# Block attention and two MLPs on one core: where the weights are converted, where s and b are applied, and how the first softmax is normalised

## Chip, cores and metric

The kernel runs on one core of a Trainium2 chip. The metric is the device time of one execution in microseconds. Before the change it is 1034.1 us, the median of three runs (1032.76 to 1035.13).

## What is computed

Attention in blocks of 64 positions (4 batches, 8 heads, 576 positions, head size 64), whose output of 2304 tokens by 512 passes through two MLPs with 2048 hidden columns. The weights arrive as float64 words and are used as fp32.

```python
scores = scale * q @ k.T; masked where block_i < block_j; attn = softmax(scores)
x = attn @ v                                   # 2304 tokens x 512
h = x @ w_in;  g = s * relu(h)**2 + b;  x = g @ w_out        # first MLP, s and b are scalars
h = x @ w_in2; g = max(0.01 * h, h);    out = g @ w_out2     # second MLP
```

## The kernel before, in words

Nothing is kept in bf16: every fp32 operand of the MLPs is split into a high part (rounded to the type `float32r`) and a low part (the rest), and each product is three matmuls: high by high, low by high, high by low. Tokens are cut into five groups of positions, k = 0 to 4 (four of 128 positions by 4 batches, 512 columns, and one of 64 by 4, 256 columns). A block is one group through one MLP; ten blocks run in the order 0, 1, 2, 4, 3 for the first MLP and 0, 1, 2, 3, 4 for the second (`ORDER`). A block has 16 units (`NF`), one for each 128 hidden columns, and a unit is `m_in` (12 matmuls into the PSUM bank `h`), four element-wise operations on ACT and DVE, and `m_out` (12 matmuls into the four banks `y0` to `y3`).

The order of the work is written by a planner: `Graph.add` registers a step with the engines that it may run on and a cost for each, its predecessors, the buffers that it opens and uses, and a due time; `Graph.order` simulates the engines and always starts the ready step with the earliest due time that has its buffers. The steps are then issued in that order, so each engine's queue, SP's for the DMAs included, is a fixed sequence. A step that may run on several engines goes to the first that is idle in that simulation, DVE before ACT. `port=True` keeps two such steps from overlapping on DVE and POOL.

Attention of the first group runs ahead of everything, as four head pairs: two scores banks per pair, `softmax` (L382: maximum, exp with its sum, reciprocal, and one normalising multiplication per column group, L422, on POOL or DVE), `transposed` (L436, through the one bank `t`) and the product with v into the bank `s`. The attention of each later group (`later_block`, L541) is spread over the block before it, in 16 units of one head pair and one batch.

First weights (`first_weights`, L301): each chunk f has two halves of 512 KB, w_in and w_out. Chunks 0 to 14 load both halves as words into a buffer of the pool `w` (L312), chunk 15 through the single buffer `raw` (L320). `convert` (L259) turns a half into fp32 in a buffer `u` of the pool `st`: ACT scales the high words (L264), DVE shifts (L268), puts in the sign (L272) and the low bits (L278), all with a contiguous result. `split` (L288) makes the high part on ACT (L290) and the low part on POOL or DVE (L293). Second weights (`second_weights`, L327): during blocks 0 to 3, half by half through `raw` and `u`, stored to DRAM as fp32 (`w2s`, L340), and loaded again (L348) and split while block 4 and block 5 run. The 16 buffers of the pool `w` hold raw first words, the first weights and then the second weights.

In the first MLP (L703 to L711) a unit's four operations are Relu on ACT, `s * r * r` on DVE with the scalar read from `s_sb`, `+ b` with the rounding to the high part on ACT with the scalar from `b_sb`, and the low part on DVE with `b_sb` again. `h` has one bank in the first MLP and three (`s`, `s`, `t`) in the second. `x_split` (L661) splits a block's input; for the second MLP it loads it from `yT`, which the first MLP's outputs were written to.

Of the kernel before, what the change touches and what calls it, by code (L numbers as in the profile page):

```python
# [43 lines left out]
class Graph:  # L44
# [22 lines left out]
    def order(self):  # L67
# [90 lines left out]
def act(n, ptr=0, acc=False):  # L158
    return 0.19 + n / 1200 + 0.09 * ptr + 0.2 * acc
# [15 lines left out]
def kernel(  # L175
# [23 lines left out]
    scale = 1.0 / float(D) ** 0.5  # L199
    EARLY = NF - 1  # L200
# [4 lines left out]
    def ps(name, bufs):  # L205
# [5 lines left out]
        "w": (sb("w", NF), NF), "st": (sb("st", 3), 3), "raw": (sb("raw", 1), 1),  # L211
# [3 lines left out]
        "sm": (sb("sm", 8), 8),  # L215
# [3 lines left out]
    G = Graph({k: n for k, (_, n) in pools.items()}, ("k", "v", "p", "pt", "s", "t", "h", "xf", "xh", "xl", "st", "raw"))  # L219
# [8 lines left out]
    id_sb = const.tile([128, 128], F32, name="id_sb")  # L228
    s_sb = const.tile([128, 1], F32, name="s_sb")
# [3 lines left out]
    w2s = dr_p.tile([NF, 2, 128, 512], F32, name="w2s")  # L233
# [3 lines left out]
    att_pe = [16 * (share[k] * 1.64e-3 + 2 * (k + 1) * 0.16 + 0.2) for k in range(NB)]  # L237
# [21 lines left out]
    def convert(raw, view, loaded, due):  # L259

        u = buf("st", [128, 512], F32, "u")

        def up(e):
            e.activation(out=u(), in_=view()[:, :, 1].bitcast(F32), func=ACTF.Copy, scale=2.0 ** -112)  # L264

        def shift(e):
            ui = u().bitcast(I32)
            e.tensor_scalar(out=ui, in0=ui, scalar1=3, scalar2=None, op0=ALU.logical_shift_left)  # L268

        def sign(e):  # L270
# [5 lines left out]
        def low(e):
            ui = u().bitcast(I32)
            e.scalar_tensor_tensor(  # L278
                out=ui, in0=view()[:, :, 0], scalar=29, in1=ui, op0=ALU.logical_shift_right, op1=ALU.bitwise_or
            )  # L280

# [539 lines left out]
```

## Time and profile before

| | us |
|---|---|
| median of three runs | 1034.1 (1032.76 to 1035.13) |
| the profiled execution | 1033.27 |
| its span | 1031.4 |
| PE busy | 996.7 |
| DVE busy | 484.6 |
| ACT busy | 392.6 |
| POOL busy | 144.1 |

The span is the stretch that the profile covers, 1.9 us shorter than the execution's own time. Busy time is the union of an engine's instructions. Matmuls are pipelined and their ends are modelled, so a busy PE can still be one that goes slowly: how long a block takes tells more. L695 and L734 are the MLPs' matmuls, L430 and L602 the scores, L445 the transposes, L639 and L519 the products with v.

### The profile page before, as it was taken

How to read it: one execution, taken by the hardware profiler on the slowest of the kernel's cores; microseconds unless marked ns; L12 is line 12 of the kernel's file. 1: busy time of each engine (PE TensorE's matmuls, PEld its weight loads, DVE VectorE, ACT ScalarE, POOL GpSimd, SP SyncE). 2: the span in 40 equal slices, each digit the busy share in tenths (PEclk: the TensorE clock that was granted, in tenths of full speed). 3: DMA queues.
4: the chain of work that ended last, by engine and by line, in shares of the span. 5: the costliest groups of instructions: out<-in, count | busy, mean ns of one | idle time of the engine just before them, and what ended most of it. 6: DMA issues, size and time to landing. Idle time of an engine off the chain costs nothing.

```text
span 1031.4 us, 14803 instructions
## 1 busy us (share of the span) xinstructions
PE 996.7 (97%) x5520; PEld 810.6 (79%) x5520; DVE 484.6 (47%) x956; ACT 392.6 (38%) x893; POOL 144.1 (14%) x268
## 2 busy tenths in 40 slices
PE   6799998999999999999999999999999999999997
PEld 5577776787777777777788888888888888888897
DVE  4688877656666676567664544113111211311221
ACT  4555654434444443355443445123212211321221
POOL 3445543101121111022220000000000000000000
PEclk8899999999999999999999999999999999999999
DMA  6455652544536656355624233001000200200011
GB/s 170 137 166 173 192 155 89 159 122 130 167 103 176 190 171 191 99 154 156 185 77 149 91 103 102 1 1 56 27 1 1 82 1 1 62 1 1 1 41 22
DMA packets 97607, 100.66 MB, mean 98 GB/s; under 512 B 29312, under 2 KB 72448, under 8 KB 97536
## 3 DMA queue, kind: packets, MB, share of 16 engines
q1 hardware_dynamic: 95904, 99.19, 32.7%
q8 instruction: 44, 0.72, 0.3%
q10 hardware_dynamic: 1632, 0.52, 0.2%
q14 instruction: 27, 0.22, 0.1%
HBM read 81.86 MB, written 17.83 MB: 97 GB/s over the span
## 4 chain that ended last, share of the span: by engine, by line
PE 90%; DVE 3%; ACT 2%; DMA 2%; POOL 1%; SPq 1%; issue 1%; ACTq 0%; DVEq 0%; POOLq 0%
PE h L695 37%; PE y L734 37%; PE s L430 5%; PE t L445 4%; PE o L639 4%; PE s L602 2%; DMA early<-in_moe_w_in_dram 1%; POOL p L422 1%; ACT g L706 1%; DMA fq<-in_q_dram 1%; DVE pt L372 0%; DVE g L707 0%; DVE u L272 0%; SPq L561 0%; ACT p L408 0%
## 5 line engine op out<-in xcount | busy, mean ns | idle before, releaser
L695 PE MATMUL h<-xh,w 128*128 128x512 f32 (+1 forms) x1280 | 452.9, 384 | 4.4 <-ACT g L706 3.2
L734 PE MATMUL y<-gh,w 128*128 128x512 f32 (+1 forms) x1280 | 372.4, 374 | 4.0 <-ACT gh L709 3.2
L695 PEld LDWEIGHTS h<-xh,w 128*128 128x128 f32 x1280 | 237.7, 189 | 56.6 <-ACT g L706 8.8
L734 PEld LDWEIGHTS y<-gh,w 128*128 128x128 f32 x1280 | 230.4, 189 | 47.6 <-ACT gh L709 5.0
L734 PE MATMUL y<-gl,w 128*128 128x512 f32 (+1 forms) x640 | 237.0, 370 | 0.5 <-DVE gl L715 0.2
L695 PE MATMUL h<-xl,w 128*128 128x512 f32 (+1 forms) x640 | 236.1, 369 | 0.0
L715 DVE TENSOR_TENSOR gl<-g,gh 128x512 fp32r<-128x512 f32 (+1 forms) x80 | 51.1, 639 | 294.8 <-ACT g L714 294.8
L713 ACT ACTIVATE gh<-h 128x512 fp32r<-128x512 f32 (+1 forms) x80 | 44.4, 554 | 289.2 <-PE h L695 289.2
L734 PEld LDWEIGHTS y<-gl,w 128*128 128x128 f32 x640 | 120.8, 189 | 23.2 <-DVE gl L710 2.3
L695 PEld LDWEIGHTS h<-xl,w 128*128 128x128 f32 x640 | 121.1, 189 | 21.8 <-issue 2.8
L706 ACT ACTIVATE g<-h 128x512 f32<-128x512 f32 (+1 forms) x80 | 44.3, 554 | 125.2 <-PE h L695 117.3
L422 POOL TENSOR_SCALAR p<-p,l 128x64 f32<-128x64 f32 (+7 forms) x128 | 72.0, 578 | 107.3 <-DVE l L417 75.0
L707 DVE SCALAR_TENSOR_TENSOR g<-g,s_sb 128x512 f32<-128x512 f32 (+1 forms) x80 | 56.4, 705 | 57.7 <-ACT g L706 57.0
L445 PE MATMUL t<-id_sb,p 128*128 128x128 f32 x400 | 68.7, 284 | 8.6 <-DVE pt L372 3.7
L408 ACT ACTIVATE p<-s,nm 128x64 f32<-128x64 f32 (+7 forms) x128 | 62.8, 504 | 36.4 <-DVE nm L402 24.9
L445 PEld LDWEIGHTS t<-id_sb,p 128*128 128x128 f32 x400 | 49.4, 144 | 29.8 <-POOL p L422 7.4
L430 PE MATMUL s<-k,qz 128*128 128x192 f32 (+2 forms) x192 | 69.5, 466 | 2.9 <-ACT p L408 2.9
L399 DVE TENSOR_REDUCE nm<-s 128x1 f32<-128x192 f32 (+3 forms) x104 | 52.8, 522 | 30.7 <-PE s L430 30.4
L709 ACT ACTIVATE gh<-g,b_sb 128x512 fp32r<-128x512 f32 (+1 forms) x80 | 54.1, 677 | 31.0 <-DVE g L707 30.8
L710 DVE SCALAR_TENSOR_TENSOR gl<-g,b_sb,gh 128x512 fp32r<-128x512 f32 (+1 forms) x80 | 57.1, 713 | 15.0 <-ACT gh L709 14.8
L372 DVE COPY pt<-t 128x512 f32<-128x512 f32 (+2 forms) x60 | 37.5, 625 | 40.3 <-PE t L445 40.2
L293 POOL TENSOR_TENSOR w<-u,w 128x512 fp32r<-128x512 f32 x32 | 43.5, 1358 | 58.5 <-ACT w L290 52.3
(52 smaller groups left out, 718.3 us busy)
## 6 DMA issues: line engine op xcount, KB each, us to landing
raw<-in_moe_w_in_dram SPq DMA_DIRECT2D x17, 512.0 KB, 4.6
raw<-in_moe_w_out_dram SPq DMA_DIRECT2D x17, 512.0 KB, 4.0
w2s<-u SPq DMA_DIRECT2D x32, 256.0 KB, 4.4
v<-in_v_dram SPq DMA_DIRECT2D x32, 256.0 KB, 3.5
wf<-w2s SPq DMA_DIRECT2D x16, 512.0 KB, 3.6
early<-in_moe_w_in_dram SPq DMA_DIRECT2D x15, 512.0 KB, 4.1
early<-in_moe_w_out_dram SPq DMA_DIRECT2D x15, 512.0 KB, 4.2
k<-in_k_dram SPq DMA_DIRECT2D x32, 144.0 KB, 3.4
```

The source lines that it names most:

```text
L399: e.reduce_max(out=nm()[:, j:j + r], in_=i, axis=AX.X)
L408: e.activation(out=P()[:, pcols[j]:pcols[j] + n], in_=bk()[:, c:c + n], func=ACTF.Exp, bias=nm()[:, j:j + 1], scale=scale, accum_out=l()[: ...
L422: e.tensor_scalar(out=pp, in0=pp, scalar1=l()[:, j:j + 1], scalar2=1.0, op0=ALU.mult, op1=ALU.mult)
L430: e.matmul(out=bk()[:, c:c + n], lhsT=q_ap(j), rhs=k_ap(j, n), start=True, stop=True)
L445: e.transpose(tb()[:, x * 128:(x + 1) * 128], P()[:, pc:pc + 128], id_sb)
L695: e.matmul(out=h()[:, :T], lhsT=w()[:, wi, c * 128:(c + 1) * 128], rhs=x[blk, c]()[:, :T], start=(c == 0 and n == 0), stop=(c == KD - 1 an ...
L706: a = G.add({"ACT": act(T)}, lambda e: e.activation(out=g()[:, :T], in_=h()[:, :T], func=ACTF.Relu), [prev], [g], [h], due)
L707: a = G.add({"DVE": dve(T)}, lambda e: e.scalar_tensor_tensor(out=g()[:, :T], in0=g()[:, :T], scalar=s_sb, in1=g()[:, :T], op0=ALU.mult, o ...
L709: hi = G.add({"ACT": act(T, 1)}, lambda e: e.activation(out=gh()[:, :T], in_=g()[:, :T], func=ACTF.Identity, bias=b_sb), [a], [gh], [g], due)
L710: lo = G.add({"DVE": dve(T)}, lambda e: e.scalar_tensor_tensor(out=gl()[:, :T], in0=g()[:, :T], scalar=b_sb, in1=gh()[:, :T].bitcast(F32), ...
L715: lo = G.add({"DVE": dve(T)}, lambda e: e.tensor_tensor(out=gl()[:, :T], in0=g()[:, :T], in1=gh()[:, :T].bitcast(F32), op=ALU.subtract), [ ...
L734: e.matmul(out=y()[:, :T], lhsT=w()[:, wi, d * 128:(d + 1) * 128], rhs=x()[:, :T], start=(f == 0 and n == 0), stop=(f == NF - 1 and n == 2),)
```

## The change

First and second weights: a chunk's two halves are converted together, in instructions of 1024 columns, in place in the buffer of raw words (`chunk`): DVE shifts the low words, puts the sign of the high words into them, ACT scales the high words, DVE shifts them and joins the two, ACT makes the high part, DVE the low part. Low words and high words alternate in memory, so each of these reads, and all but the last two write, every second word. Chunk 0 stays in halves. Chunk 15 goes in halves through two buffers of the pool `pt`; the pool `raw` is gone. Loads of chunks 0 to 14 carry an earliest time of 6.0 + 4.9 f us for the planner. The second weights no longer go through DRAM: they are loaded and converted as `w` buffers come free in block 4, at most three chunks ahead, each due 25 us before its use.

First MLP: a unit is Relu on ACT, the square (ACT, or DVE as g * h with h from PSUM), the rounding on ACT and the low part on DVE, without scalars. s is a scale on the evacuation of the outputs. b is taken through the weights: group 4 carries two more columns, of ones in the high part and zeros in the low (set by two POOL copies per unit), its outputs there give the column sums of w_out, and b times those, `c_sb`, is added in the second MLP's `x_split`. Block 4 uses three banks for `h`.

Start: the exp table is loaded by a dummy exp, eight matmuls run on zeros ahead of the data, k is loaded before q, ACT's queue issues the loads of three pairs instead of two, the third pair's scores have banks of their own, the transposes alternate between the banks `t` and `h`, the product with v goes to `t`, the third and fourth pair's probabilities lie in a `w` buffer, and the normalisation is two `tensor_tensor` operations on DVE, of 256 and 512 columns, with the reciprocal broadcast. Further, the planner's costs change by a few hundredths of a us.

```diff
+    WARM, LATE, PACE, AHEAD = 8, 10, (6.0, 4.9), 3
...
+    def chunk(w, raw, layer, f, lds, halves, at0, due):
+        r, rr, n = slice(halves[0], halves[-1] + 1), slice(halves[0] - at0, halves[-1] + 1 - at0), len(halves)
+        parts = lambda s, dt: w().bitcast(dt).rearrange("p (i s) n -> p i s n", s=2)[:, r, s]
+        word = lambda s: raw()[:, rr, :, s]
+        def low(e):
+            e.tensor_scalar(out=word(0), in0=word(0), scalar1=29, scalar2=None, op0=ALU.logical_shift_right)
+        def sign(e):
+            e.scalar_tensor_tensor(out=word(0), in0=word(1), scalar=-(1 << 31), in1=word(0), op0=ALU.bitwise_and, op1=ALU.bitwise_or)
         def up(e):
+            e.activation(out=word(1).bitcast(F32), in_=word(1).bitcast(F32), func=ACTF.Copy, scale=2.0 ** -112)
         def shift(e):
+            e.scalar_tensor_tensor(out=word(1), in0=word(1), scalar=3, in1=word(0), op0=ALU.logical_shift_left, op1=ALU.bitwise_or)
         def hi(e):
+            e.activation(out=parts(0, F32R), in_=word(1).bitcast(F32), func=ACTF.Copy)
         def lo(e):
+            e.tensor_tensor(out=parts(1, F32R), in0=word(1).bitcast(F32), in1=parts(0, F32), op=ALU.subtract)
...
     def second_weights():
+            raw = buf("w", [128, 2, 512, 2], I32, "early")
+            lds = [w_load(1, f, i, raw, i, [opened[f - AHEAD] if f >= AHEAD else w_ok[0, NF - 1, 1]], [raw] * (i == 0), due - 6, 0) for i in range(2)]
+            opened.append(chunk(w, raw, 1, f, lds, [0, 1], 0, due))
...
     def softmax(k, banks, cols, P, pcols, due, after):
+        if k == 0:
+            for j in range(0, ns, 4):
+                def fn(e, j=j):
+                    pp = P()[:, 128 * j:128 * j + 512].rearrange("p (r n) -> p r n", r=4)[:, :, :cols[j][2]]
+                    e.tensor_tensor(out=pp, in0=pp, in1=l()[:, j:j + 4].unsqueeze(2).to_broadcast([128, 4, cols[j][2]]), op=ALU.mult)
...
     def x_split(blk, c):
+            hi = G.add({"ACT": act(T)}, lambda e: e.activation(out=h()[:, :T], in_=xf()[:, :T], func=ACTF.Identity, bias=cc), [*ok, *c_ok], [h], [xf], due)
...
     def m_in(blk, f):
-        h = bank("h" if layer == 0 else ("s", "s", "t")[f % 3], "h")
+        h = bank("h" if blk < NB - 1 else ("s", "s", "t")[f % 3], "h")
...
-            a = G.add({"DVE": dve(T)}, lambda e: e.scalar_tensor_tensor(
-                out=g()[:, :T], in0=g()[:, :T], scalar=s_sb, in1=g()[:, :T], op0=ALU.mult, op1=ALU.mult), [a, *sb_ok], [], [g], due, port=True)
-            hi = G.add({"ACT": act(T, 1)}, lambda e: e.activation(out=gh()[:, :T], in_=g()[:, :T], func=ACTF.Identity, bias=b_sb), [a], [gh], [g], due)
+            a = G.add(both(T), square, [a], uses=[g, h], due=due)
+            hi = G.add({"ACT": act(T)}, lambda e: e.activation(out=gh()[:, :T], in_=g()[:, :T], func=ACTF.Copy), [a], [gh], [g], due)
...
+            if k == NB - 1:
+                hi = G.add({"POOL": 0.15}, lambda e: e.tensor_copy(out=gh()[:, T:T + 2], in_=ones[:, 0:2]), [a, ones_ok], [], [gh], due)
+                lo = G.add({"POOL": 0.15}, lambda e: e.tensor_copy(out=gl()[:, T:T + 2], in_=ones[:, 2:4]), [hi, lo, ones_ok], [], [gl], due)
```

## Rows read from the trace of the kernel before

**Rows 1.** The page: its part 1, busy time of each engine with its share of the span and its instructions; the first line of its part 4, the chain that ended last by engine.

```profile
PE 996.7 (97%) x5520; PEld 810.6 (79%) x5520; DVE 484.6 (47%) x956; ACT 392.6 (38%) x893; POOL 144.1 (14%) x268
...
PE 90%; DVE 3%; ACT 2%; DMA 2%; POOL 1%; SPq 1%; issue 1%; ACTq 0%; DVEq 0%; POOLq 0%
```

**Rows 2.** The table by stretches: start and end in us, length, then busy us and instructions (x) of PE, PEld, DVE, ACT and POOL, the granted clock, the busy share of the DMA engines and GB/s. The borders are those at which a new block's 192 first matmuls begin.

```profile
0.00:41.00 41.00, 28.69 (x170) 22.80 (x171) 19.76 (x42) 18.10 (x76) 16.04 (x49) 0.79 0.60 164
41.00:182.80 141.80, 129.97 (x682) 97.58 (x680) 113.58 (x236) 82.75 (x192) 65.86 (x88) 0.99 0.51 153
182.80:302.10 119.30, 119.24 (x648) 94.82 (x648) 72.00 (x149) 51.11 (x112) 19.31 (x39) 1.00 0.48 138
...
542.70:628.20 85.50, 84.81 (x374) 69.80 (x374) 42.48 (x64) 37.62 (x64) 0.00 (x0) 1.00 0.33 108
628.20:715.20 87.00, 87.00 (x386) 72.06 (x385) 17.92 (x27) 24.55 (x44) 0.00 (x0) 1.00 0.08 28
```

**Rows 3.** The chain of waits inside three stretches (41 to 182.8, 302.1 to 429.9 and 429.9 to 542.7 us, in this order): the share of the stretch that each engine and line has in it.

```profile
by line: PE h L695 21.6%; PE y L734 19.8%; PE s L430 7.5%; DMA early<-in_moe_w_in_dram 6.3%; PE o L639 4.7%; PE t L445 4.2%; issue 3.2%; DVE g L707 3.0%; DVE u L272 3.0%; POOL p L422 2.8%; SPq L555 2.7%; DVE u L278 2.5%; ACT g L706 2.5%; PO
...
by line: PE h L695 34.2%; PE y L734 33.4%; PE s L602 12.3%; PE o L639 7.3%; PE t L445 7.3%; DMA qz<-in_q_dram 1.7%; POOL p L621 1.0%; ACT g L706 0.9%; SPq L561 0.8%; DVE nm L606 0.4%; issue 0.3%; DVE u L268 0.3%; DVE nm L610 0.2%
...
by line: PE y L734 24.3%; PE s L430 23.3%; PE h L695 19.7%; PE o L639 14.7%; PE t L445 12.8%; ACT g L706 1.4%; ACT pt L370 1.0%; issue 1.0%; DVE xl L678 0.6%; ACT xh L676 0.6%; DVE pt L372 0.5%; ACT p L408 0.3%; ACTq L706 0.1%
```

**Rows 4.** The timeline of the first 45 us, engine by engine (ACT, DVE, POOL, PE): start and length in us, engine, line, operation, what it writes and reads, how many in a row, and in brackets the idle time before it with what ended it.

```profile
10.69 1.28 ACT L408 ACT_TABLE_LOAD   x1 [10.69 <-DMA fq<-in_q_dram]
...
7.89 0.42 DVE L399 TENSOR_REDUCE nm<-s 128x4 f32<-128x256 f32 x1 [4.81 <-PE s L430]
...
40.27 0.69 DVE L529 TENSOR_TENSOR xl<-o,xh 128x512 fp32r<-128x512 f32 x1 [0.17 <-ACT xh L527]
...
15.42 2.58 POOL L422 TENSOR_SCALAR p<-p,l 128x64 f32<-128x64 f32 x8 [11.37 <-ACT p L408]
...
32.52 2.58 POOL L422 TENSOR_SCALAR p<-p,l 128x64 f32<-128x64 f32 x8 [1.38 <-ACT w L290]
...
5.92 6.54 PE L430 MATMUL s<-fk,fq 128*128 128x64 f32 x32 [5.92 <-DMA fq<-in_q_dram]
...
18.69 1.12 PE L445 MATMUL t<-id_sb,p 128*128 128x128 f32 x4 [0.79 <-DVE pt L372]
...
21.65 1.93 PE L430 MATMUL s<-fk,fq 128*128 128x64 f32 x14
```

**Rows 5.** Groups of instructions in block 0 (41 to 182.8 us) on DVE and POOL: line, engine, operation, tiles and shapes, count, busy us, mean ns of one, idle time before them and what ended it.

```profile
L278 DVE SCALAR_TENSOR_TENSOR u<-early,u 128x512 int32<-128x512 int32 x28 | 22.1, 790 | 0.1
...
L268 DVE TENSOR_SCALAR u<-u 128x512 int32<-128x512 int32 x29 | 14.6, 504 | 1.3 <-ACT u L264 1.3
...
L414 DVE TENSOR_SCALAR l<-l 128x2 f32<-128x2 f32 x20 | 8.6, 430 | 4.0 <-ACT p L408 4.0
L402 DVE TENSOR_SCALAR nm<-nm 128x2 f32<-128x2 f32 x21 | 7.2, 342 | 0.4
...
L293 POOL TENSOR_TENSOR w<-u,w 128x512 fp32r<-128x512 f32 x30 | 40.9, 1363 | 58.5 <-ACT w L290 52.3 <-DVE u L272 3.6 <-DMA qz<-in_q_dram 1.6
```

**Rows 6.** The tiles `early` and `u` (first weights as loaded, and their converted half): duration in ns, least, median and longest, of one instruction of a line.

```profile
L272 DVE SCALAR_TENSOR_TENSOR u<-early,u x30: 678/684/954, 29.7 to 165.3; 128x512 int32<-128x512 int32 x30
L278 DVE SCALAR_TENSOR_TENSOR u<-early,u x30: 676/684/1770, 30.4 to 166.1; 128x512 int32<-128x512 int32 x30
...
L268 DVE TENSOR_SCALAR u<-u x64: 375/420/1514, 26.4 to 517.3; 128x512 int32<-128x512 int32 x64
```

**Rows 7.** SP's queue in the timeline (start us, length, line, operation), twice two DMAs that follow each other on it.

```profile
27.90 0.51 SPq L312 DMA_DIRECT2D early<-in_moe_w_in_dram  x1
40.58 1.14 SPq L561 DMA_DIRECT2D k<-in_k_dram  x2
...
159.53 0.43 SPq L320 DMA_DIRECT2D raw<-in_moe_w_in_dram  x1
172.09 0.33 SPq L320 DMA_DIRECT2D raw<-in_moe_w_out_dram  x1
```

**Rows 8.** Groups in blocks 1 to 3 (182.8 to 542.7 us) on DVE and ACT, columns as in rows 5.

```profile
L272 DVE SCALAR_TENSOR_TENSOR u<-raw,u 128x512 int32<-128x512 int32 x32 | 25.9, 809 | 0.9
...
L278 DVE SCALAR_TENSOR_TENSOR u<-raw,u 128x512 int32<-128x512 int32 x32 | 22.9, 715 | 0.7
...
L268 DVE TENSOR_SCALAR u<-u 128x512 int32<-128x512 int32 x32 | 14.8, 463 | 6.5 <-ACT u L264 3.7 <-DMA k<-in_k_dram 2.4
...
L402 DVE TENSOR_SCALAR nm<-nm 128x2 f32<-128x2 f32 x27 | 5.5, 202 | 0.7
...
L414 DVE TENSOR_SCALAR l<-l 128x2 f32<-128x2 f32 x28 | 4.7, 166 | 9.8 <-ACT p L408 9.7
...
L264 ACT ACTIVATE u<-raw 128x512 f32<-128x512 f32 x32 | 21.2, 663 | 11.7 <-DMA raw<-in_moe_w_out_dram 5.5 <-DMA raw<-in_moe_w_in_dram 5.0 <-DMA w2s<-u 0.7
```

**Rows 9.** Groups around the border of the two MLPs (542.7 to 715.2 us) on DVE and ACT, columns as in rows 5.

```profile
L293 DVE TENSOR_TENSOR w<-wf,w 128x512 fp32r<-128x512 f32 x32 | 21.3, 688 | 6.1 <-ACT w L290 6.1
...
L707 DVE SCALAR_TENSOR_TENSOR g<-g,s_sb 128x512 f32<-128x512 f32 x16 | 12.0, 750 | 31.8 <-ACT g L706 31.8
...
L715 DVE TENSOR_TENSOR gl<-g,gh 128x512 fp32r<-128x512 f32 x15 | 10.4, 692 | 63.6 <-ACT g L714 63.6
L706 ACT ACTIVATE g<-h 128x512 f32<-128x512 f32 x16 | 9.6, 598 | 34.8 <-PE h L695 34.7
```

More of the change, by code (lines that the diff above doesn't have):

```diff
@@ L274, in sign @@
             )
[L276 to L280, printed above, removed]
-        a = G.add({"ACT": 0.66}, up, [loaded], [u], [raw], due)
-        a = G.add({"DVE": dve(512, 2)}, shift, [a], uses=[u], due=due, port=True)
-        a = G.add({"DVE": dve(512)}, sign, [a], uses=[u, raw], due=due, port=True)
-        a = G.add({"DVE": dve(512)}, low, [a], uses=[u, raw], due=due, port=True)
@@ L298, in w_tile @@
-    def w_tile(layer, f):
-        return buf("w", [128, 4, 512], F32R, "w")
+            e.tensor_tensor(out=parts(1, F32R), in0=word(1).bitcast(F32), in1=parts(0, F32), op=ALU.subtract)
+        a = G.add({"DVE": dve(512 * n, 2)}, low, lds, uses=[raw], due=due, port=True)
+        a = G.add({"DVE": dve(512 * n)}, sign, [a], uses=[raw], due=due, port=True)
+        a = G.add({"ACT": act(512 * n)}, up, [a], uses=[raw], due=due)
+        a = G.add({"DVE": dve(512 * n)}, shift, [a], uses=[raw], due=due, port=True)
@@ new lines, in chunk, with w_load @@
+        last = w_ok.get((layer, f - 1, 0)) if layer == 0 else None
+        h = a = G.add({"ACT": act(512 * n)}, hi, [a, last], [w] * (halves[0] == 0), [w, raw], due)
+        a = G.add({"DVE": dve(512 * n)}, lo, [a], uses=[w, raw], due=due, port=True)
+        for i in halves:
+            w_ok[layer, f, i] = a
+        return h
+    def w_load(layer, f, i, raw, k, after, opens, due, rel):
+        return G.add(
+            {"SP": 0.65}, lambda e: e.dma_start(out=raw()[:, k], in_=words(layer, f, i)),
+            after, opens, [raw], due, nbytes=524288, rel=rel,
+        )
@@ L432, in scores @@
             fresh.add(bk)
[L433 removed]
+            out.append(G.add({"PE": max(n * 1.67e-3, 0.214) + 0.02}, fn, after, new, [bk, *q, *kk], due - 5))
         return out
@@ L455, in transposed @@
         return done
+    tiny = G.add({"DVE": 0.1}, lambda e: memz(e, warm), due=-95)
+    G.add({"ACT": 1.4}, lambda e: e.activation(out=warm, in_=warm, func=ACTF.Exp), [tiny], due=-94)
+    wb = bank("h", "warm")
+    for i in range(WARM):
+        G.add(
+            {"PE": 0.43}, lambda e: e.matmul(out=wb()[:, :128], lhsT=qz[0][:, 0].rearrange("d h c -> d (h c)"),
+                                             rhs=qz[0][:, 0].rearrange("d h c -> d (h c)"), start=True, stop=True),
+            [qz_ok[0]], [wb] * (i == 0), [wb], -90,
+        )
     fq = [buf("w", [128, 2, B, 2, 2, 64], F32, "fq") for _ in range(2)]
```

201 lines of the change are left out of this document (98 added, 103 removed).

## The prediction

> **What bounds the kernel now.** The page first: PE is busy 97% of the span and the chain that ended last is 90% PE [rows 1], so only the places where that chain leaves PE can pay. The table by stretches finds them [rows 2]. From 542.7 us on there is almost nothing: blocks 4 and 5 take 85.5 and 87.0 us with PE busy for 84.8 and 87.0. Block 1 (182.8 to 302.1) is PE-bound too: 119.3 us, PE busy 119.24 [rows 2]. Block 0, the same 192 first matmuls and no heavier attention, takes 141.8 us, 22.5 more, and its chain is only 57.8% PE (21.6 + 19.8 + 7.5 + 4.7 + 4.2); the rest is weight loads, conversions, POOL and queue issue [rows 2, 3]. Ahead of it stand 41 us of loads and first softmax at a mean granted clock of 0.79 [rows 2]. Blocks 2 and 3 leave PE for about 5.5% and 5.0% of their chains: 7 and 5.6 us [rows 3]. So some 13 us lie in blocks 2 and 3, 22.5 in block 0, and an unknown part of 41 in the start.
>
> Durations are those of the profiled execution: 1033.27 us, 1.9 over its span of 1031.4 and 0.8 under the median of 1034.1. The sum is made on the span.
>
> **Start (0 to 41 us).** The four head pairs follow each other at 5.7 us: POOL's row of eight normalisations begins at 15.42 for the first and at 32.52 for the fourth [rows 4]. The path through a pair is exp, five of those POOL operations, four transposes, a PSUM copy, four more transposes that wait 0.8 us for that copy (one bank), AV, then the next scores, which use the banks of the pair two before. The change cuts this in four places. (a) The table load at 10.69 (1.28 us) moves ahead of the data: -1.3. (b) Eight POOL operations (2.58 us) become two on DVE. I price them by DVE's rows of the same sizes, 0.42 and 0.69, so 1.1; but the first transposes need only five of the eight (five eighths of 2.58, 1.6), so it is -0.5 per pair. (c) Two banks for the transposes: -0.8 per pair. (d) The third pair's scores go to banks of their own and no longer queue behind AV. What then sets the pace is DVE: per pair two reduces, four small operations, the norm, one or two copies and the low part, 0.42 + 0.69 + 0.8 + 1.1 + 1.0 + 0.69 = 4.7 us. Three periods of 4.7 for 5.7: -3.0; with (a) and the first pair's share of (b) and (c), -1.3: -5.6. Against it, ACT's queue now holds three more DMA issues and the early exp between its first and second issue, so the first pair's q lands later by the table load and its wait, +1.4. For it, eight warm-up matmuls: the first 32 score records take 6.54 us, 0.20 each, the later 14 take 1.93, 0.14 each [rows 4], so up to 1.9 for the first pair. I set these two against each other and take **-6** (0 if DVE, which also gets the first chunk's conversion here, keeps the old pace; -10 if all four add).
>
> **Block 0.** Each chunk of weights (two halves) costs DVE today 2 x (0.42 + 0.684 + 0.684) = 3.6 us at the median of clean instructions [rows 6] and POOL two low parts of 1.36. After, the low parts move to DVE, in instructions of 1024 columns. A clean 512-column instruction is 0.684, so 1024 columns add 512 / 0.96 = 0.53: 1.22. The one-source shift is 0.42, so 0.69 at double rate. A chunk is 0.69 + 3 x 1.22 = 4.35. DVE is busy 113.6 of 141.8 us, 80% [rows 2]. From that: some 15 us of it is excess over the clean durations (28 x 0.11 on L278, 29 x 0.08 on L268, 20 x 0.26 on L414, 21 x 0.14 on L402, and a rest on the other operations) [rows 5, 6, 8]. I read it as DVE held by POOL, whose 30 low parts run 40.9 us here, and it goes with them. That leaves 98. Conversions: 28 halves of three clean instructions, 50 us, become 14 chunks of 4.35, 61: +11. The MLP's two scalar operations, 15 x 2 x 0.75 [rows 9], become one of 0.69 and, a third of the time, a square of 0.69 (the planner may put it on ACT): -8.6. DVE's work is then 100 us, and at the same 80% share the block takes 126: **-16**. The floor is PE's own 119 (-23). The other end: the shift loses its double rate (+0.53 x 14 / 0.8 = 9) and DVE's share falls, and nothing is won (0).
>
> Two things speak for the better part of this. Loads: SP issues one at 27.90 us, then nothing at all until a key load at 40.58, and weight loads have 6.3% of block 0's chain, 9 us [rows 3, 7]. Loads are now paced by 4.9 us a chunk for the planner, ahead of a consumption of about 7.5, so the same standstill finds weights already there. And the last chunk's two halves used one buffer, loads at 159.5 and 172.1 [rows 7]; they now have two. Those two are `pt` buffers, so the next attention units wait for them a few us, behind MLP matmuls. The `h` bank is held through the square, 0.7 us longer; 12 output matmuls lie between two uses of it, 12/384 of a block's 87.0 us, 2.7, so I cost it at nothing; without that cover it would be 0.7 per unit.
>
> **Blocks 1 to 3.** Out go 32 halves of the second weights, 63.6 us of DVE and 21.2 of ACT [rows 8], and 32 loads, 32 stores and 16 reloads on SP's queue. Of the 13 us off PE in blocks 2 and 3, 2.2 are q loads and some are POOL; I take a third as conversions' share, -5. In comes a POOL copy on the path from `gl` to the output matmuls of block 3, twice 16, of two columns each: between nothing and, with a wait like a 128x2 operation of DVE at each end, 0.17 twice [rows 8], 16 x 0.34 = 5; I take +1 since units wait for PE more than for `gl`. The two extra columns are nothing. Together **-4** (0 to -10).
>
> **The MLPs' border.** All 16 second chunks are now converted between the first freed weight buffer (about 550) and 690. DVE has 42.5 + 17.9 busy of 172.5 us there [rows 2]; less 21.3 of today's low parts [rows 9] and 9 of scalar forms, plus 16 x 4.35 = 70: 100, or 58%. Spread, it is hidden: the MLP's chain of four operations (0.60 + 0.69 + 0.60 + 0.69) has the three banks that block 4 now gets. Packed one chunk per 5.44 us unit, DVE needs 4.35 + 0.69 = 5.04, still under it, but `gl` queues behind 1.22 us at a time. The loads wait on SP for freed buffers, ahead of block 5's x loads, which are due 20 us early. I take **+2** (0 to +10). The scale and the constant c sit on evacuations and x splits that exist already: nothing; c is ready 87 us before its use.
>
> **Sum:** -6 - 16 - 4 + 2 = -24. Span 1007.4, execution 1009.3, median **1010**.
>
> **Rivals.** (1) **The work only changes engine.** DVE takes the low parts over, loses the shift's double rate on the strided words, and block 0 stays near 137 to 142 us; the start and blocks 1 to 3 still pay. 1010 + 11 to 16: about 1024. For it: DVE was at 80% already. Against: POOL's holds go.
>
> (2) **Strided words in place.** The sign and the shift now read two operands and write one, all at every second word. If such streams run at half rate, each is 2 x 1.07 + 0.15 = 2.3, and with a single-rate shift a chunk is 1.22 + 2 x 2.3 + 1.22 = 7.0, 2.7 more. Block 0: 14 x 2.7 = 37 more DVE, 138 us, at 90% share 153: +11. Border: 7.0 + 0.69 = 7.7 against 5.44 per unit, 16 x 2.3 = 36 if packed, 20 with the spread. Start -4, blocks 1 to 3 -4: 1034 + 23 = 1057, slower. It decides from about 1 us more per chunk, 25%. Against it: today's sign and low operations read one such operand at 0.684, as fast as the contiguous low part of the second weights, 0.688 [rows 6, 9]. For it: no row has a strided result. [...]
>
> (3) **The gain is given back:** the border costs 10, the new order stalls elsewhere, and the time is about 1032.
>
> **How the numbers follow.** Forecast 0.6, its own range 998 to 1020; (1) 0.2; (2) 0.12; (3) 0.08, of which half lies within 0.2% (about 2 us, what a measurement here can tell from no change) and most of the rest above. Faster: 0.6 + 0.2 = 0.8; same 0.05; slower 0.15. The range reaches down to 992 (all good ends, -41, are 18 us lower and unlikely together) and up to 1036, over (1) and (3); it leaves out (2) and the best ends.
>
> **What would show it.** Fourth low part of the first block at about 35 us instead of 40.96; block 0 near 126 us with DVE near 100 busy; sign and shift at 1.22 and the one-source shift at 0.69; blocks 4 and 5 still 172 to 175 us. Wrong if those instructions last 2 us, if block 0 keeps 140, or if PE waits for `gl` at the border.

## The result, and the profile after

The changed kernel takes **1016.7 us** (median of four runs, 1014.97 to 1019.93) against 1034.0 in the same comparison: 0.984 of it [0.981, 0.987], 17 us less. Forecast were 1010, range 992 to 1036; that range takes in 1034, so a time inside it says little, and the parts of the sum have to be checked one by one. The profiled execution is the longest of the four, 1019.93 us with a span of 1018.1. Further down a second profile of the same kernel (span 1014.2) is used as the control.

The page's part 1 and the first line of its chain, as in [rows 1]; then the table by stretches, as in [rows 2], cut where a block's first matmuls begin (start, block 0, block 1, block 3, block 4, block 5).

```profile
PE 995.8 (98%) x5536; PEld 816.7 (80%) x5536; DVE 452.9 (44%) x855; ACT 403.9 (40%) x866; POOL 93.3 (9%) x238
...
PE 92%; DVE 3%; ACT 2%; DMA 1%; issue 1%; POOL 0%; ACTq 0%; SPq 0%; DVEq 0%; POOLq 0%
```

```profile
0.00:40.00 40.00, 30.64 (x181) 27.06 (x181) 23.85 (x50) 20.34 (x81) 4.32 (x17) 0.75 0.88 259
40.00:160.00 120.00, 117.07 (x629) 93.00 (x627) 95.70 (x174) 79.58 (x156) 22.91 (x48) 1.00 0.41 132
160.00:289.60 129.60, 129.46 (x713) 101.45 (x712) 56.33 (x132) 51.26 (x125) 20.47 (x48) 1.00 0.24 67
...
414.40:528.70 114.30, 110.03 (x875) 87.75 (x874) 59.36 (x141) 46.74 (x121) 27.84 (x78) 1.00 0.31 88
528.70:614.50 85.80, 85.80 (x386) 71.29 (x386) 64.64 (x79) 52.08 (x70) 0.00 (x0) 1.00 0.50 174
614.50:701.90 87.40, 87.30 (x385) 71.96 (x385) 37.30 (x48) 35.30 (x53) 0.00 (x0) 1.00 0.19 67
```

The converting instructions, as in [rows 6] (least, median and longest ns), in the order of the chain but for ACT's two:

```profile
L263 DVE TENSOR_SCALAR early<-early x31: 418/689/697, 24.4 to 636.1; 128x1024 int32<-128x1024 int32 x29, 128x512 int32<-128x512 int32 x2
L266 DVE SCALAR_TENSOR_TENSOR early<-early x31: 679/1220/1229, 25.1 to 636.9; 128x1024 int32<-128x1024 int32 x29, 128x512 int32<-128x512 int32 x2
...
L274 DVE SCALAR_TENSOR_TENSOR early<-early x31: 684/1220/1228, 29.6 to 639.3; 128x1024 int32<-128x1024 int32 x29, 128x512 int32<-128x512 int32 x2
...
L282 DVE TENSOR_TENSOR w<-early,w x31: 635/1224/1432, 32.3 to 641.7; 128x1024 fp32r<-128x1024 f32 x29, 128x512 fp32r<-128x512 f32 x2
```

That is 0.69 and three times 1.22 us, as priced. The price took 0.96 columns per ns; measured, 512 columns more take 0.536 us where two operands are read (1.220 against 0.684 [rows 6]), 0.955 per ns, and 0.269 in the one-source shift (0.689 against 0.420 [rows 6]). The fourth low part of the first block, 40.27 to 40.96 us before [rows 4], is here:

```profile
40.06 0.69 DVE L540 TENSOR_TENSOR xl<-o,xh 128x512 fp32r<-128x512 f32 x1 [0.17 <-ACT xh L538]
```

With that as the first border and block 4's first matmul (542.7 us before) as the second, the span divides like this:

| us | predicted | first profile | control |
|---|---|---|---|
| start, to the end of the fourth low part | -6 | -0.2 (40.75) | -2.6 (38.37) |
| blocks 0 to 3 from there | -16 - 4 | -13.7 (to 528.8) | -15.3 (to 524.8) |
| block 4 to the end | +2 | +0.6 | +0.7 |
| span | -24 | -13.3 | -17.2 |

Blocks 0 and 1 can't be compared by length: the new plan moves some attention from block 0 into block 1 (682 PE instructions before and 629 now, against 648 and 713). So I use **lost time**: over a stretch, the sum of the distances between the starts of successive matmuls, less the sum of the distances that the same shapes have when nothing holds them (227 ns for 512 columns of an MLP matmul, 120 for 256, and so on). With the undisturbed distances taken a little otherwise the sums shift by up to 2 us, their differences between kernels by up to 1.5. Lost time is 24.8 us before and 9.7 now in block 0, -15.1. In blocks 1, 2, 3 it was 3.5, 7.3, 9.6 and is 4.5, 5.0, 12.6: 20.4 before and 22.1 now, +1.7. The control gives the same figures within 0.1. Block 0 paid for nearly all of it: behind block 0's first matmul the span is 994.8 us before and 978.2 now, 17 less, while that matmul itself starts at 36.6 us before and at 40.0 now (36.4 in the control).

### The profile page after: what moved, and what is told of

The parts are those of the page before. It is cut to its first block, busy times and chain, and to the rows that moved or that the text cites. A ratio compares the mean times of both kernels' runs of the same rounds, so it can differ in the third digit from the quotient of the medians.

```text
span 1018.1 us, 14594 instructions
## 1 busy us (share of the span) xinstructions
PE 995.8 (98%) x5536; PEld 816.7 (80%) x5536; DVE 452.9 (44%) x855; ACT 403.9 (40%) x866; POOL 93.3 (9%) x238
## 4 chain that ended last, share of the span: by engine, by line
PE 92%; DVE 3%; ACT 2%; DMA 1%; issue 1%; POOL 0%; ACTq 0%; SPq 0%; DVEq 0%; POOLq 0%
PE h L716 38%; PE y L765 37%; PE s L430 6%; PE o L650 4%; PE t L445 4%; PE s L613 2%; PE o L530 1%; ACT p L400 1%; DVE nm L391 0%; DVE g L732 0%; POOL p L422 0%; DMA fk<-in_k_dram 0%; ACT g L734 0%; ACT w L279 0%; DMA fq<-in_q_dram 0%
## 5 line engine op out<-in xcount | busy, mean ns | idle before, releaser
L765 PE MATMUL y<-gh,w 128*128 128x512 f32 (+2 forms) x1280 | 369.4, 372 | 0.1
L765 PE MATMUL y<-gl,w 128*128 128x512 f32 (+2 forms) x640 | 236.2, 369 | 0.2 <-DVE gl L745 0.2
L745 DVE TENSOR_TENSOR gl<-g,gh 128x512 fp32r<-128x512 f32 (+1 forms) x80 | 51.0, 638 | 271.5 <-ACT g L744 271.5
L716 PEld LDWEIGHTS h<-xl,w 128*128 128x128 f32 x640 | 121.0, 189 | 21.3 <-issue 2.6
L422 POOL TENSOR_SCALAR p<-p,l 128x192 f32<-128x192 f32 (+3 forms) x95 | 59.0, 634 | 189.5 <-DVE l L409 136.0
L732 DVE TENSOR_TENSOR g<-g,h 128x512 f32<-128x512 f32 (+1 forms) x52 | 32.8, 630 | 64.2 <-ACT g L734 63.8
L358 ACT ACTIVATE pt<-t 128x512 f32<-128x512 f32 (+2 forms) x67 | 33.7, 502 | 64.6 <-PE t L445 63.9
L360 DVE COPY pt<-t 128x512 f32<-128x512 f32 (+2 forms) x53 | 34.0, 641 | 52.0 <-PE t L445 51.6
L737 DVE TENSOR_TENSOR gl<-g,gh 128x512 fp32r<-128x512 f32 (+1 forms) x80 | 51.0, 637 | 11.7 <-ACT gh L736 10.2
L736 ACT ACTIVATE gh<-g 128x512 fp32r<-128x512 f32 (+1 forms) x80 | 47.1, 588 | 16.1 <-DVE g L732 14.6
```

Source lines behind the costliest of these rows:

```text
L422: e.tensor_scalar(out=pp, in0=pp, scalar1=l()[:, j:j + 1], scalar2=1.0, op0=ALU.mult, op1=ALU.mult)
L716: e.matmul(out=h()[:, :T], lhsT=w()[:, wi, c * 128:(c + 1) * 128], rhs=x[blk, c]()[:, :T], start=(c == 0 and n == 0), stop=(c == KD - 1 an ...
L736: hi = G.add({"ACT": act(T)}, lambda e: e.activation(out=gh()[:, :T], in_=g()[:, :T], func=ACTF.Copy), [a], [gh], [g], due)
L737: lo = G.add({"DVE": dve(T)}, lambda e: e.tensor_tensor(out=gl()[:, :T], in0=g()[:, :T], in1=gh()[:, :T].bitcast(F32), op=ALU.subtract), [ ...
L745: lo = G.add({"DVE": dve(T)}, lambda e: e.tensor_tensor(out=gl()[:, :T], in0=g()[:, :T], in1=gh()[:, :T].bitcast(F32), op=ALU.subtract), [ ...
L765: e.matmul(out=y()[:, :W], lhsT=w()[:, wi, d * 128:(d + 1) * 128], rhs=x()[:, :W], start=(f == 0 and n == 0), stop=(f == NF - 1 and n == 2),)
```

## Experiments

Each is an edit of the changed kernel. Since the start of one and the same kernel varies by some 4 us from run to run (block 0's first matmul at 40.0 and at 36.4 us), the table gives what can be read apart from it: the end of the fourth low part, the lost time in block 0 and in blocks 1 to 3, and the span behind block 0's first matmul, which the first profile and the control have at 978.2 and 977.8.

| run | median us | ratio to before | 4th low part | lost, block 0 | lost, 1 to 3 | span behind |
|---|---|---|---|---|---|---|
| e0_after (control) | 1017.0 | 0.983 [0.981, 0.985] | 38.4 | 9.7 | 22.1 | 977.8 |
| e2_no_warm | 1016.7 | 0.983 [0.981, 0.986] | 40.0 | | | 977.8 |
| e3_third_first | 1014.6 | 0.981 [0.978, 0.983] | 39.0 | 9.5 | 21.6 | 977.1 |
| e1_hold | 1021.3 | 0.987 [0.985, 0.989] | 43.6 | | | 978.7 |
| e1b_hold_few | 1015.6 | 0.983 [0.981, 0.984] | 35.2 | | | 977.8 |
| e7b_lo_on_pool | 1028.2 | 0.994 [0.992, 0.996] | 40.2 | 19.1 | 22.2 | 987.5 |
| e10_late_loads | 1058.5 | 1.024 [1.022, 1.027] | 42.4 | 49.7 | 21.7 | 1019.2 |
| e4b_square_gg | 1016.7 | 0.983 [0.982, 0.985] | 38.9 | 10.3 | 18.5 | 975.2 |
| e5_no_b | 1018.4 | 0.985 [0.984, 0.987] | 39.4 | 9.6 | 21.3 | 977.2 |
| e6_second_before | 1017.0 | 0.984 [0.982, 0.987] | 40.4 | 9.5 | 21.2 | 977.1 |
| e8_sb_in_unit | 1017.4 | 0.984 [0.982, 0.986] | 40.2 | 9.3 | 21.0 | 976.5 |
| e9_hold_and_square | 1012.2 | 0.980 [0.978, 0.981] | 36.3 | 10.4 | 18.4 | 974.9 |

The medians come from three sets of runs, in which the kernel before took 1034.8 us (e0 to e3 and e1_hold), 1033.9 (e1b, e4b, e5, e7b) and 1032.9 (e6, e8, e9, e10). Across sets only the ratios can be compared, and a microsecond between two medians there says nothing.

### The start

Three theories of why the start gained so little: the order of the work on TensorE (A), TensorE's granted clock, which is 0.50 from 13.5 to 23.7 us of the first profile (B), VectorE and the loads (C).

**Control**

> The changed kernel once more, word for word, as the kernel to compare the next ones with on the same chip. Every theory expects 1015 to 1020 us; its start (to the first m_in matmul) 40 us, block 0 about 120 us, blocks 1 to 3 about 369 us together. If the clock sets the spread between executions, the start's length here goes with the length of its half-clock stretches: 20 us of them gave a start of 40.0 us in the first profile.

Same time, but another start: 36.4 us to the first m_in matmul instead of 40.0. TensorE's timeline at the first scores, in the first profile and in the control:

```profile
5.75 5.86 PE L430 MATMUL s<-fk,fq 128*128 128x64 f32 x32 [0.87 <-DMA fq<-in_q_dram]
```

```profile
5.36 2.02 PE L430 MATMUL s<-fk,fq 128*128 128x64 f32 x16 [0.58 <-DMA fq<-in_q_dram]
8.65 2.03 PE L430 MATMUL s<-fk,fq 128*128 128x64 f32 x16 [1.27 <-DMA fq<-in_q_dram]
```

In the control they start 112 ns apart from the first on. In the first profile the first 20 are 214 ns apart and the rest 112, with the same warm-up ahead, and the clock's column (last but two) does not show it:

```profile
0.00:13.00 13.00, 9.64 (x48) 9.18 (x48) 4.46 (x9) 3.94 (x18) 3.98 (x15) 1.00 0.72 178
```

The column counts time without an entry in the trace's list of clock changes as full speed. The first entry of that list, full speed, begins at 10.05 us in the first profile, where the 21st score matmul starts, and at 4.53 us in the control, ahead of all scores.

**No warm-up**

```diff
-    WARM, LATE, PACE, AHEAD = 8, 10, (6.0, 4.9), 3
+    WARM, LATE, PACE, AHEAD = 0, 10, (6.0, 4.9), 3
```

> The changed kernel without its eight warm-up matmuls. Theory B expects the first scores at half clock from the first matmul on, the first exponential 1 to 2 us later and the start 1 to 2 us longer; theories A and C expect the start within 1 us, since the first loads set the first scores and the third pair's exponentials the end.

Its first 20 score matmuls are 214 ns apart, the first exponential starts at 10.2 us, as in the first profile (10.5) and 1.8 later than in the control (8.4). The median is the control's. So the warm-up saves about 2 us up to the first exponential in an execution in which it works, and it does not always work: of the twelve profiles with it, the first exponential starts at 8.4 to 8.5 us in eight and at 10.2 to 10.5 in four.

**Third pair's scores first**

```diff
-        tr = transposed(P, pcols, cells, pt, nrm, due, ("t", "h"))
+        tr = transposed(..., also=first_sc[2][1][-1:] if p == 0 else [])   # all scores planned ahead of this loop
```

> The changed kernel with one change of order in the start: the 18 score matmuls of the third pair of heads are put ahead of the first pair's transposes on TensorE, so they don't wait for the first pair's softmax. Theory A (the third pair's scores stand behind the first pair's transposes in TensorE's order, so ScalarE has nothing to exponentiate from 19.5 to 24.25 us): the third pair's exponentials start at 18 to 20 us instead of 24.74, the fourth low part of the first block is done 3 to 5 us earlier than 40.06, and the time falls by 3 to 5 us. Theory B (the half clock of TensorE in the start costs it): the idle time before the first transposes shrinks, the clock may stay up longer, but the start shortens by 1 to 2 us only. Theory C (loads and VectorE set the pace): the fourth low part stays at 40 us within 1 us, and the time with it.

The third pair's exponentials do start at 17.5 us instead of 23.1, but the first pair pays: its low part starts at 22.5 instead of 19.4, and the fourth ends at 39.0 instead of 38.4. Theory A falls. The median is 2.4 us under the control's, with overlapping intervals; whether that is a gain stays open.

**TensorE kept busy**

```diff
+        if p == 0:   # behind the second pair's scores
+            for i in range(12): matmul(out=wb()[:, :128], lhsT=zz(), rhs=zz())
+        if p == 2:   # behind the third pair's scores (first trial only)
+            for i in range(24): matmul(out=wc()[:, :128], lhsT=zz(), rhs=zz())
```

> The changed kernel, its order otherwise kept, with 36 matmuls of no use in TensorE's gaps of the start (12 behind the second pair's scores, 24 as filler behind the third pair's), so that TensorE is not idle from 11.6 to 14.4 us. Theory B (the half clock of 13.5 to 23.7 us costs the start): the granted clock stays at full speed there, the groups of transposes, scores and AV behind it run in half their time (t 2.2 to 1.1, s 4.1 to 2.05, o 2.0 to 1.0 us), and the start falls by 3 to 5 us. Theory A (order) and theory C (loads, VectorE): the clock stays up but the start changes by less than 1 us, since ScalarE's and VectorE's chains set it. If the filler stands in the way, the start grows by up to 36 x 0.06 = 2 us.

A miss of the experiment's making: the 24 fillers read a buffer that a q load writes, waited for that load, and held the third pair's transposes until 33.5 us. Up to there it went as theory B says: second low part at 23.8 instead of 26.4. So again, with the first twelve alone:

> The changed kernel with twelve matmuls of no use on TensorE behind the second pair's scores, and none of the 24 fillers that the first trial of this had. Theory B (the half clock of 13.5 to 23.7 us costs the start): the clock stays up until about 20 us, the second low part of the first block comes 2 to 3 us earlier than at 26.4, as it did with the fillers (23.8), the fourth at 35 to 36 instead of 37.7, and the time is 1014 to 1015 us. Theory C (VectorE, which is busy without a gap from 26 us on, sets the end of the start): the second low part comes earlier, the fourth stays at 37 to 38 us, and the time is 1016 to 1018 us.

The stretch of 16 to 22 us (length, busy us of PE, PEld, DVE, ACT, POOL, then granted clock, DMA) in the first profile and in this one:

```profile
16.00:22.00 6.00, 6.00 (x36) 5.55 (x35) 2.80 (x7) 1.19 (x2) 0.15 (x1) 0.50 0.90 277
```

```profile
16.00:22.00 6.00, 5.84 (x58) 5.23 (x54) 3.82 (x10) 3.27 (x17) 0.15 (x1) 1.00 0.92 288
```

At a granted clock of 0.50 TensorE gets through 36 matmuls, at 1.00 through 58. Ahead of it, it had been idle from 11.6 to 14.4 us in the first profile, and its granted clock fell to 0.50 at 13.5. The fourth low part ends at 35.2 us, 3.2 before the control's: theory B is shown for this execution. Of the 3.2 us, 2.0 are won up to the first low part and 1.2 on the way to the second; from there on the low parts follow each other as in the control (5.8 and 5.6 us against 5.7 and 5.6). And the profiled execution is the fastest of four that spread from 1012.9 to 1016.9 us: by the ratios (0.983 and 0.983) the median gains nothing.

For theory C, the last part of the start, up to the fourth low part, in the control and before:

```profile
26.00:38.37 12.37, 8.67 (x60) 6.66 (x61) 11.91 (x25) 9.54 (x28) 0.00 (x0) 0.86 0.86 259
```

```profile
26.00:41.00 15.00, 11.41 (x68) 7.96 (x67) 9.11 (x21) 7.70 (x25) 6.84 (x20) 0.66 0.45 150
```

VectorE is busy for 96% of it now and was for 61%: it took over GpSimd's normalising and low parts, and some 7 us of conversions stand in its row there. What they hold up can be read at the fourth pair in the control: its product with v, its high part and its low part, and what stands ahead of these two on ScalarE and VectorE.

```profile
34.78 1.15 PE L530 MATMUL o<-pt,fv 128*64 128x128 f32 x16
...
35.70 1.17 ACT L271 ACTIVATE early<-early 128x1024 f32<-128x1024 f32 x1
...
36.55 1.22 DVE L266 SCALAR_TENSOR_TENSOR early<-early 128x1024 int32<-128x1024 int32 x1
...
36.72 0.64 ACT L538 ACTIVATE xh<-o 128x512 fp32r<-128x512 f32 x1
...
37.68 0.69 DVE L540 TENSOR_TENSOR xl<-o,xh 128x512 fp32r<-128x512 f32 x1
```

The product is done at 35.93 us, the high part starts 0.8 us later, behind a conversion on ScalarE, and the low part 0.3 us after the high part's end, behind one on VectorE: 1.1 us of the start are seen to go to conversions here. Fewer conversions in this stretch were seen in e10_late_loads alone, where the fourth pair's product with v was put behind the first m_in matmuls and ended later; so how much of the start the conversions cost in all is not settled.

### Block 0

```diff
-        a = G.add({"DVE": dve(512 * n)}, lo, [a], uses=[w, raw], due=due, port=True)
+        on = {"POOL": pool(512 * n, True)} if layer == 0 and f % 2 else {"DVE": dve(512 * n)}
+        a = G.add(on, lo, [a], uses=[w, raw], due=due, port=True)
```

> The changed kernel with the low parts of every second chunk of the first weights on GpSimd (1024 columns each, seven of them in block 0), as all of them were before in halves. Theory (GpSimd's operations hold VectorE, and that was block 0's loss): 7 x 2.7 = 19 us of GpSimd come back, half of what was there; VectorE's other operations get longer by some 7 us in all while its own work falls by 8.5; block 0 grows by 4 to 10 us, the time to 1021 to 1027. Rival (earlier loads and whole chunks are what paid, and the low parts' engine is of no weight): block 0 stays within 2 us of 120.

Block 0: 130.0 us, lost time 19.1 instead of 9.7, the span behind its first matmul 9.7 us longer. The groups of VectorE's two small softmax operations and of the low parts (count, busy us, mean ns of one, idle time before), first in the control's block 0, then with seven low parts on GpSimd, from 42 to 170 us:

```profile
L406 DVE TENSOR_SCALAR l<-l 128x2 f32<-128x2 f32 x16 | 2.8, 176 | 3.2 <-ACT p L400 2.9
L394 DVE TENSOR_SCALAR nm<-nm 128x2 f32<-128x2 f32 x16 | 2.7, 172 | 0.2
```

```profile
L395 DVE TENSOR_SCALAR nm<-nm 128x2 f32<-128x2 f32 x15 | 8.2, 549 | 0.2
L407 DVE TENSOR_SCALAR l<-l 128x2 f32<-128x2 f32 x16 | 6.6, 413 | 7.0 <-ACT p L401 5.4 <-POOL w L282 1.5
...
L282 POOL TENSOR_TENSOR w<-early,w 128x1024 fp32r<-128x1024 f32 x7 | 17.6, 2514 | 47.7 <-ACT w L279 27.2 <-DMA early<-in_moe_w_in_dram 20.5
```

The two-column operations last two to three times as long, though nothing of theirs was changed. Of these 31, the eight that overlap a low part on GpSimd last 157 to 2414 ns, six of them 910 or more, and the other 23 last 155 to 364. The hold is shown. That all of the 10 us is the hold's is not: TensorE's matmuls also wait for GpSimd itself in this block, for a low part (2.51 us on GpSimd, 1.22 on VectorE) and for its normalising multiplications, neither of which stands among the waits of the control's matmuls there (us in total, times, longest):

```profile
PE t L446 <- POOL p L423: 3.2, 4, 1.6
PE h L717 <- POOL w L282: 1.8, 1, 1.8
```

```diff
-                w_load(0, f, i, raw, i, [first_done] if f >= LATE else [], [raw] * (i == 0), due - 30, PACE[0] + PACE[1] * f)
+                w_load(0, f, i, raw, i, [prev] + ([first_done] if f >= 11 else []), [raw] * (i == 0), due - 30, 0)   # prev: the load before
```

> The changed kernel with the first weights' loads as before: each chained to the one before it, without the pace of 4.9 us a chunk, so that the second chunk's loads come after the attention's. Theory (what block 0 gained is GpSimd's hold on VectorE alone, as the low parts on GpSimd suggest: +10.4 us for half of them): block 0 stays at 119 to 122 us and the start loses or gains no more than 1 us. Rival (half of the gain is from the earlier loads, which had 9 us of block 0's chain before): block 0 grows by 5 to 9 us. Theory C of the start (early conversions take VectorE's time there) also expects the fourth low part of the first block 2 to 4 us earlier than 37.7 to 40.1.

Neither forecast: block 0 takes 162.2 us, 42.6 more, and the kernel is **26 us slower than the one before the change** (1058.5 against 1032.9 in this comparison). Planned one at a time, the loads stand singly between the attention's on SP's queue, as they did before, and those wait for buffers (22 us for matmuls between 42 and 114 us). Issues of three weight loads in the first part of block 0:

```profile
93.47 0.58 SPq L297 DMA_DIRECT2D early<-in_moe_w_in_dram  x1
...
98.62 0.58 SPq L297 DMA_DIRECT2D early<-in_moe_w_out_dram  x1
...
103.33 0.58 SPq L297 DMA_DIRECT2D early<-in_moe_w_in_dram  x1
```

From 47.1 to 110.3 us it is one in 5.3 us, 10.5 us a chunk. In the kernel before it was one in 4.8 us (25 from 44.6 to 158.9), 9.5 a chunk, and its block 0 went at 9.1 a unit: its loads alone could have set that pace. The control has issued all 30 by 77.9 us. Of the 49.7 us lost here, 16 are lost up to 114 us and 34 behind it, when all but four loads have been issued: there a unit takes some 10 us, in an order planned for late loads, in which ScalarE converts just ahead of the unit's own operations and TensorE waits:

```profile
engine line waited for: us in total, times, longest us
PE y L766 <- ACT gh L737: 14.5, 7, 2.9
```

So the gain needs both earlier loads and fewer low parts on GpSimd. How much of the 42.6 us is the loads' pace and how much the order that the planner wrote for late loads, no run takes apart. Early loads with the old conversion by halves were not tried.

### Blocks 1 to 3

In block 3 of the control TensorE (1.0 us) and its weight loads (3.5 us) wait for the bank `h` until the square has read it; before, the bank was released by the first operation on it.

```diff
-                    e.tensor_tensor(out=g()[:, :T], in0=g()[:, :T], in1=h()[:, :T], op=ALU.mult)
+                    e.tensor_tensor(out=g()[:, :T], in0=g()[:, :T], in1=g()[:, :T], op=ALU.mult)
-            a = G.add(both(T), square, [a], uses=[g, h], due=due)
+            a = G.add(both(T), square, [a], uses=[g], due=due)
```

> The changed kernel with the square reading the evacuated copy twice, instead of the copy and the bank `h`, so that `h` is free after the first operation on it. Theory (TensorE's first matmuls wait for `h` through the square: 3.5 us of weight loads and 1.0 us of matmuls in block 3 behind L732, none before): block 3 falls from 114.3 to 110 to 112 us, blocks 1 and 2 by 0 to 1 each, the time to 1012 to 1014 us. Rival (these waits only stand where the softmax of blocks 1 to 3 would be waited for anyway): the waits behind L732 go, those behind L400 and L360 grow, and the time stays within 1.5 us of 1017.

Lost time in block 3 falls from 12.6 to 9.4 us (9.6 before the change), over blocks 1 to 3 by 3.6 (block 0 loses 0.6 more); the span behind the first m_in matmul by 2.6. The start of the profiled run took back 1.7, and the median, at the control's ratio, is where the rival had it. How it goes is not quite as I wrote. Waits in block 3, control first:

```profile
PE s L430 <- ACT p L400: 1.6, 4, 0.7
PE t L445 <- ACT pt L358: 1.0, 3, 0.3
PE h L716 <- DVE g L732: 1.0, 1, 1.0
```

```profile
PE h L716 <- ACT g L734: 1.8, 2, 1.2
PE t L445 <- POOL p L422: 0.2, 1, 0.2
```

TensorE still waits for `h`, now for the relu; the waits for the softmax and the transposes' copies are what went. I read it so, without a run that shows it alone: the planner, which sees `h` free earlier, puts matmuls of the MLP where it had waited for the attention.

```diff
-            if k == NB - 1:     # ones and zeros behind gh and gl, two POOL copies per unit
+            if False:
...
-        W = T + 2 * (layer == 0 and k == NB - 1)
+        W = T
```

> The changed kernel without b: no columns of ones, none of their 32 copies on GpSimd, no product for the constant, which is zero (the output lacks what b adds). Theory (the copies stand between `gl` and the second matmuls of block 3 and cost what block 3 got worse): block 3 falls by 2 to 4 us. Rival (the held bank or the softmax): block 3 stays within 1 us of 114.3, and everything else as it is.

Without b the two extra columns go too. Block 3 loses 11.8 instead of 12.6: copies and columns cost 0.8 us.

```diff
-            opened.append(chunk(w, raw, 1, f, lds, [0, 1], 0, due))       # in blocks 4 and 5
+            u, a = convert(raw, raw, ld, due)                             # a half at a time, in blocks 0 to 3
+            spilled[f, i] = G.add({"SP": 0.65}, lambda e: e.dma_start(out=w2s[f, i], in_=u()), [a], ...)
```

> The changed kernel with the second weights converted half by half during blocks 0 to 3, stored and loaded again, as before; the rest as changed. Theory of the prediction (these conversions cost blocks 1 to 3 about 5 us, their removal to the border costs 2): blocks 1 to 3 grow by 4 to 6 us in all, the border falls by 0 to 2, the time is 1019 to 1022 us. Rival (VectorE is busy for half of these blocks only and the planner fits the conversions in; the held bank `h` is what kept the gain from showing): blocks 1 to 3 within 1.5 us of 368.6, the border the same within 0.5, the time 1015 to 1019 us.

The rival: lost time 21.2 instead of 22.1 with all 32 conversions back, and the same time. They cost blocks 1 to 3 nothing.

```diff
-            a = G.add(both(T), square, [a], uses=[g, h], due=due)
+            a = G.add({"DVE": dve(T)}, lambda e: e.scalar_tensor_tensor(out=g, in0=g, scalar=s_sb, in1=g, op0=mult, op1=mult), ...)
+            hi: activation(Identity, bias=b_sb);  lo: scalar_tensor_tensor(scalar=b_sb, op0=add, op1=subtract)
```

> The changed kernel with s and b back in the first MLP's unit: relu, then VectorE's product with the scale, ScalarE's copy plus b, VectorE's scalar form of the low part; no ones and no constant, and the bank `h` free after the relu. Theory (the held bank cost the blocks 2.5 us and the shorter operations won block 0 some): block 3 falls to 109 to 111 us, block 0 grows by 3 to 9 us with VectorE's 0.3 us more in each of two operations of 16 units, the time is 1018 to 1024 us. Rival (VectorE has room in block 0 once GpSimd no longer holds it): block 0 stays within 2 us, and the time is 1013 to 1016 us, faster than with s and b moved.

Block 0 loses 9.3 instead of 9.7, blocks 1 to 3 21.0 instead of 22.1; the span behind the first m_in matmul is 1.3 us shorter and the time the same. As it was done, moving s and b out of the unit won nothing. But this kernel also frees `h` after the relu and has no copies of ones. Against e4b_square_gg, which frees `h` too, its span behind the first m_in matmul is 1.3 us longer (976.5 against 975.2): so much the move is worth where the bank is freed, and in the change the held bank takes it back.

### Both gains together

e1b_hold_few and e4b_square_gg in one kernel, with ten warm-up matmuls.

> The changed kernel with both gains put together: twelve matmuls of no use behind the second pair's scores and ten instead of eight at the front, so that TensorE's clock stays up, and the square reading the copy twice, so that `h` is free after the relu. If the two add (2 to 3 us in the start where the clock holds, 2.5 us in block 3): start 33 to 37 us, span behind the first m_in matmul 975 instead of 978 us, the time 1010 to 1013 us. If the clock's hold is lost anyway, 1014 to 1015 us.

**1012.2 us** (1011.5 to 1012.8), the fastest here. By the ratios (0.980 and 0.983) that is some 3.6 us under the control, with intervals that just touch; of the 3.8 us between the two profiled spans (1010.4 and 1014.2), 2.9 lie behind block 0's first matmul and 0.9 ahead of it. Block 3 in its table:

```profile
409.90:519.20 109.30, 107.04 (x842) 85.82 (x841) 56.58 (x138) 47.95 (x125) 29.34 (x79) 1.00 0.31 89
```

It holds 842 matmul records and not 875 as in the first profile, 32 of the missing ones products with v that the new order put elsewhere; so the 5.0 us by which it is shorter overstate the gain, which by lost time in blocks 1 to 3 is 3.7.

## Why the prediction was right in sign and 7 us off

- **Start, -6: failed.** The step that failed is "Three periods of 4.7 for 5.7". Low parts follow each other at 7.0, 5.7 and 5.6 us in the control (7.4, 5.7, 6.3 in the first profile). The sum of 4.7 left out the conversions that VectorE does there; I had named them only as the bound of nothing, and the time came out near it. They are seen to cost 1.1 us at the fourth pair; that they are all that keeps the pace at 5.7 is not shown. It also left out that TensorE would go on at half its clock through the second pair (granted clock 0.50 from 16 to 22 us): without that, e1b_hold_few has 3.2 us back, but its last two periods are still 5.8 and 5.6. The first pair's part was about right: its low part starts at 19.4 to 20.7 instead of 23.2. In pricing the warm-up I took 32 score records for the first pair's, and they are two pairs'; it came out near 1.9 (1.8 up to the first exponential) by luck, since a record goes from 214 to 112 ns and not from 0.20 to 0.14 us.
- **Block 0, -16: right in size, half right in cause.** -15.1 of lost time; VectorE 95.7 us busy, forecast 100. GpSimd's hold is shown (with seven low parts back on GpSimd the block loses 10 us, part of it by waiting for GpSimd itself). But I took the loads for a bonus ("Two things speak for the better part of this"). With the loads chained again and the order that the planner writes for them, the block takes 42.6 us more: so the change is slower than the kernel before, a rival that I did not have.
- **Blocks 1 to 3, -4: failed, +1.7.** Two steps. "I take a third as conversions' share, -5": it is nothing (e6_second_before); VectorE had been busy for 72 of the 119.3 us of block 1 [rows 2], the row of block 2's chain that I had read shows 0.3% on a conversion, 0.4 us [rows 3], and removing operations that nobody waited for paid nothing. "I cost it at nothing", of the bank `h`: it is 3.6 us of lost time in blocks 1 to 3, 2.6 of the span. The cover of 2.7 us was that of 512 columns; block 3, where most of it is lost, has 256, and twelve output matmuls take 12 x 0.12 = 1.4 us there. The copies were +1 and are 0.8. With the bank and the copies taken off, blocks 1 to 3 would have gained 2.7 us, which no run gives to a part of the change.
- **Scalars out of the unit, -8.6 of VectorE:** part of block 0's sum, and worth nothing as it was done (e8_sb_in_unit). With s and b back, VectorE is busy for 102.7 of block 0's 118.5 us, against 96.7 of 119.6, and the block loses no more time: VectorE has room there.
- **Border, +2:** +0.6 in length, no lost time to speak of (1.2 us in block 4 before, 0.1 now); VectorE 102 us busy in blocks 4 and 5, forecast 100.
- **Rival (2), half rate of strided words:** excluded. The sign and the shift, with all three streams at every second word, take 1.220 us for 1024 columns, where the rival had 2.3; the one-source shift takes 0.689 for 1024 strided columns, where without its double rate it was to take 1.22.
- **Rivals (1) and (3):** neither; block 0 paid, and blocks 4 and 5 took 173.2 us together.

## What to carry to other kernels

Where a change lifts two limits at once (here loads issued singly and an engine held by another), its time shows one sum, and undoing one of them can cost more than the whole gain, as the loads did here (42.6 us of block 0), in part through the order that the planner then wrote: the loads' pace has to be read off the queue, as us per chunk, before a conversion is made coarser. Work that was taken off an engine with room, and that nobody waited for, was worth nothing here whatever its duration (with all 32 conversions back, blocks 1 to 3 lose 21.2 us instead of 22.1). The bank `h` was better released by the first operation that reads it (2.6 us of the span here); I read that as the planner's doing, which orders the work by when buffers come free.

## Not expected of the hardware

- The same program's start varies by 3.6 us (40.0 and 36.4 to block 0's first matmul): eight warm-up matmuls are followed by scores at 112 ns from the first on (control), or by 20 at 214 ns (first profile). In the first profile TensorE was idle from 11.6 to 14.4 us, its granted clock fell to 0.50 at 13.5 and stayed there until 23.7.
- The granted clock's column shows 1.00 for 0 to 13 us of the first profile, although matmuls started 214 ns apart until 10.05 us, where the trace's first clock entry begins: ahead of the first entry, their spacing tells more than the column.
